# Two score batches of 224 and 288 key columns for query tiles 3 and 4, and row sums and a PSUM tile shared by two query tiles

## The chip, the core and the metric

The kernel runs on one core of one Trainium2 chip. The metric is the device time of one execution in microseconds (us). The engines are named as in the profile: PE is TensorE's matmuls and PEld its weight loads, DVE is VectorE, ACT is ScalarE, POOL is GpSimd, SP is SyncE, which only issues DMAs here.

## The reference

Attention with a memory, and behind it a feed-forward layer with a squared ReLU. B=4 batches, H=8 heads, S=576 tokens, D=64.

```
scores = q @ k.T / sqrt(D), masked causally (keys after the query get -1e9)
a      = exp(scores - rowmax);  a /= rowsum(a) + 1e-9
local  = a @ v
phi(x) = where(x > 0, x, exp(x) - 1) + 1
mem    = (phi(q) @ M_prev) / (phi(q) @ z_prev + 1e-6)
g      = sigmoid(beta)                        # one number per head
attn   = g * mem + (1 - g) * local
x      = attn.transpose(0, 2, 1, 3).reshape(2304, 512)
out    = relu(x @ w_in) ** 2 @ w_out          # w_in 512 x 2048, w_out 2048 x 512
```

## The kernel before

Queries come in tiles: tile 0 with 64 tokens, tiles 1 to 4 with 128 each. Tile 0 of all batches is done apart, at the start. Keys of tile 3 reach to column 448, of tile 4 to 576, of tile 2 to 320 and of tile 1 to 192.

`attention()` is a generator for one unit: a batch, a pair of heads and some tiles. Batches 0 and 1 are cut into units with tiles 1 and 2 and units with tiles 3 and 4 (four of each in a batch); batches 2 and 3 have four units each with all four tiles. These are 24 units, numbered here 0 to 23. Units 0 to 2 transpose in float32 on PE (`full`), units 0 to 5 compute scores with one matmul term, the 18 from unit 6 on with three terms (high times high, low times high, high times low).

What one unit does, in the order of its lines:

- It splits q and k into high and low parts (L475 to L478), applies phi (L488 to L502), scales v into the float16 pair `vs` (L525, L528), multiplies phi(q) by the memory into `pm` and writes g times the memory's answer into `feat` (L552 to L558). `feat` is the attention's output and the feed-forward's input.
- `scores(group)` computes one batch of scores into `sps`, a PSUM tile of 2 heads by 512 columns (tag "s", one buffer). `SGROUP` says which columns of which tile form a batch, in tuples (tile, first key, last key). The matmuls are at L583. Then DVE takes each head's part of each tuple out of PSUM (L604: scale, mask, running minimum `mx`) into the float32 tile `e`. A part that doesn't begin at key 0 takes `mx` of the first part as its start (a column of one number per partition). Only when the last part is out can the next batch be written.
- For each tile in the order 2, 1, 3, 4: ACT takes the exponential of `e` in place, one instruction for each head, and writes the row's sum into `sm` (L624; a tile of 128x2, tag "sm", four buffers, one tile for each query tile). ACT makes the float16 high part of `a` (L662), DVE the low part (L664), SP issues a transposing DMA `aT<-a` (L668). DVE adds 1e-9 to `sm` and multiplies it by `vz` (L669) and takes the reciprocal (L673).
- PE multiplies `aT` by `vs` into `acc` (L688; PSUM, tag "av", two buffers, used also for `pm` and `vt`). DVE adds the product times `sm` to `feat`, once for each head (L691, 128x64).

`moe(n)` is the feed-forward for 256 tokens: 24 "up" matmuls of 256 columns for each of eight pairs of feature blocks (L973 to L975), ReLU and square on ACT (L979, L980), a float16 high part `gh` on ACT (L982) and a low part `gl` on DVE (L985), and 12 "down" matmuls of 512 columns (L944 to L946). Its input `xT` is made of `feat` by `token_halves` (L715 to L724, with a transposing DMA). The last 512 tokens go through `moe_last` (L744), after all attention; matmuls of 512 tokens into `seven` (L812 to L814, L841).

The order of instructions isn't written by hand: a scheduler with a model of times places the instructions of all generators on the engines' queues, so the feed-forward's matmuls fill PE between the attention's. Score matmuls have a high priority in it. What is queued on one engine runs in that order. A change in `attention()` therefore moves other instructions too.

Of the kernel before, what the change touches and what calls it, by code (L numbers as in the profile page):

```python
# [8 lines left out]
F32 = mybir.dt.float32  # L9
# [6 lines left out]
ALU = mybir.AluOpType  # L16
# [50 lines left out]
TORD = [2, 1, 3, 4]  # L67
SGROUP = {2: [[(2, 0, 320), (1, 0, 192)]], 1: [], 3: [[(3, 0, 448), (4, 0, 64)]], 4: [[(4, 64, 576)]]}
GB = 2
# [29 lines left out]
def fused_kernel(ctx: ExitStack, tc: tile.TileContext, t0_d, kk_d, qv_d, beta, w_in, w_out, out):  # L99
# [353 lines left out]
    def attention(b, p, tiles, ld, after, early, sfull, full, ap, ap_early):  # L453
# [113 lines left out]
        if ap_early:  # L567
            yield "whole"
        started, a12 = set(), None
        row = {}  # L570

        def scores(group):
# [20 lines left out]
            for (i, ka, kb), cs in zip(group, at_col):  # L593
                q0 = QT[i][0]
                if ka == 0:
                    row[i] = (
                        ap.tile([P, 2, S], F32, tag="e", name="e", bufs=EB if ap is at else EB2),
                        at.tile([P, 2, 2], F32, tag="mx", name="mx", bufs=4),
                        at.tile([P, 2], F32, tag="sm", name="sm", bufs=4),
                    )  # L600
                e, mx, _ = row[i]
                s = int(ka > 0)
# [12 lines left out]
        for i in [t for t in TORD if t in tiles]:  # L615
            q0, n = QT[i]
            ke = q0 + n
            for group in SGROUP[i]:
                scores(group)
            ns = 2 if any(ka for g in SGROUP[i] for t, ka, _ in g if t == i) else 1  # L620
            e, mx, sm = row.pop(i)
            for h in range(2):
# [24 lines left out]
            else:  # L647
# [20 lines left out]
                nc.sync.dma_start_transpose(out=aT[:, :, :n], in_=a[:n])  # L668
            nc.vector.scalar_tensor_tensor(  # L669
                out=sm[:n], in0=sm[:n], scalar=1e-9, in1=gm[:n, h0 : h0 + 2] if full else vz[:n],  # L670
                op0=ALU.add, op1=ALU.mult,
            )
            nc.vector.reciprocal(sm[:n], sm[:n])  # L673
            yield

            acc = ps.tile([P, 2, D], F32, tag="av", name="acc", bufs=2)
            for h in range(2):
# [9 lines left out]
                for x, (lhs, rhs) in enumerate(mms):  # L687
                    nc.tensor.matmul(acc[:n, h], lhs[:, :n], rhs, start=x == 0, stop=x == len(mms) - 1)  # L688
            for h in range(2):
                xo = memx[:n, i - 1, h]  # L690
                x = nc.vector.scalar_tensor_tensor(  # L691
                    out=xo, in0=acc[:n, h], scalar=sm[:n, h : h + 1], in1=xo, op0=ALU.mult, op1=ALU.add
                )
                step.setdefault(me, x)
            yield
# [446 lines left out]
```

## Time and profile before

| | |
|---|---|
| times of 3 runs | 562.0, 559.24, 561.57 us |
| median | 561.57 us |
| the profiled execution | 561.7 us |
| its span (first to last instruction) | 559.9 us |
| outside the span | 1.8 us |
| busy in the span | PE 522.5 us (93%), PEld 369.5 (66%), DVE 451.9 (81%), ACT 412.0 (74%), POOL 17.8 (3%) |
| mean granted clock of TensorE | 0.976 of full speed |

The page also gives the span in 40 slices of 14 us with each engine's busy tenths: up to about 136 us PE stands at 5 to 9, from there on nearly always at 9; DVE is at 8 or 9 up to 255 us, and at 6 to 8 after that; the attention ends at about 437 us, and from there to the end PE has only the feed-forward. The clock that the throttle granted PE is given in tenths of full speed in these slices and in windows as a share (1.00 is full speed).

How the rows below are to be read. A row of a timeline is a run of equal instructions: start in us from the span's start, us from the first's start to the last's end, engine, line, operation, out<-in tiles, shape and count; in square brackets the idle time of the engine before it, and what ended that. Instructions on one engine overlap at their ends, so the cost of one is read from its start to the next one's start, where the next waits for nothing.

### The profile page before, as it was taken

The page shows a single profiled execution, that of the slowest core. Times are in us where ns is not written, and L with a number is a line of the kernel's source. Part 1 is how long each engine was busy: PE and PEld are TensorE (multiplying, and loading weights), DVE is VectorE, ACT ScalarE, POOL GpSimd, SP SyncE. Part 2 cuts the span into 40 slices and gives each one's busy share as a digit, 9 for nine tenths or more (in the row PEclk, how much of TensorE's full clock was granted, in tenths as well). Part 3 has the DMA queues.
Part 4 walks back from the last instruction along what each step waited for, and adds up shares of the span by engine and source line. Part 5 has one row for each costly group of instructions (what it writes and reads, how often), then busy time and mean ns, then how long its engine had stood idle before and what let it go on. Part 6 is the DMA issues. An engine that isn't in the chain of part 4 may idle for free.

```text
span 559.9 us, 12611 instructions
## 1 busy us (share of the span) xinstructions
PE 522.5 (93%) x4767; PEld 369.5 (66%) x4767; DVE 451.9 (81%) x1421; ACT 412.0 (74%) x884; POOL 17.8 (3%) x20
## 2 busy tenths in 40 slices
PE   5655999998999999999989999999999999999996
PEld 4544766656777767667756777667766866447766
DVE  6898879998997999999967778888686788745645
ACT  3699997894788879989867777889666734566252
POOL 1000030111010000000000000000000000000000
PEclk9967999998999999999989999999999999999999
DMA  8968931497576759988746476481755320100002
GB/s 309 405 215 247 325 109 39 124 160 186 117 157 152 174 136 158 179 171 183 131 90 150 115 138 123 76 145 47 115 94 80 91 39 1 39 1 1 1 1 75
DMA packets 133132, 71.37 MB, mean 127 GB/s; under 512 B 115408, under 2 KB 121552, under 8 KB 133072
## 3 DMA queue, kind: packets, MB, share of 16 engines
q1 hardware_dynamic: 133072, 70.57, 53.7%
q8 instruction: 37, 0.61, 0.5%
q14 instruction: 23, 0.19, 0.1%
HBM read 37.53 MB, written 4.72 MB: 75 GB/s over the span
## 4 chain that ended last, share of the span: by engine, by line
PE 53%; DVE 23%; ACT 11%; DMA 9%; issue 2%; SPq 0%; POOL 0%; DVEq 0%; ACTq 0%
PE up L973 6%; PE up L974 5%; PE up L975 5%; DVE e L604 5%; PE oacc L945 5%; PE oacc L946 5%; PE oacc L944 5%; PE acc L688 4%; DVE a L664 4%; PE seven L841 4%; ACT e L624 3%; PE sp L583 3%; DMA xT<-hl 2%; PE seven L814 2%; PE seven L813 2%; PE seven L812 2%
## 5 line engine op out<-in xcount | busy, mean ns | idle before, releaser
L973 PE MATMUL up<-xT,w 128*128 128x256 f16 x448 | 124.0, 277 | 5.7 <-DMA xT<-hl 5.1
L974 PE MATMUL up<-xT,w 128*128 128x256 f16 x448 | 123.9, 277 | 0.0
L975 PE MATMUL up<-xT,w 128*128 128x256 f16 x448 | 123.8, 276 | 0.0
L624 ACT ACTIVATE e<-e,mx 128x320 f32<-128x320 f32 (+3 forms) x128 | 77.4, 606 | 40.4 <-DVE feat L691 22.3
L944 PE MATMUL oacc<-w,gh 128*128 128x512 f16 x224 | 85.2, 380 | 0.6 <-ACT gh L982 0.5
L945 PE MATMUL oacc<-w,gh 128*128 128x512 f16 x224 | 85.3, 381 | 0.0
L946 PE MATMUL oacc<-w,gl 128*128 128x512 f16 x224 | 81.6, 380 | 0.0
L664 DVE SCALAR_TENSOR_TENSOR a<-e,a 128x128 f16<-128x128 f32 x116 | 65.8, 578 | 10.4 <-ACT a L662 9.5
L662 ACT ACTIVATE a<-e 128x128 f16<-128x128 f32 x116 | 55.0, 523 | 1.8 <-DMA aT<-a 1.4
L973 PEld LDWEIGHTS <-w 128*128 128x128 f16 x448 | 44.4, 99 | 16.3 <-DMA xT<-hl 5.6
L974 PEld LDWEIGHTS <-w 128*128 128x128 f16 x448 | 44.5, 99 | 11.5 <-issue 1.1
L975 PEld LDWEIGHTS <-w 128*128 128x128 f16 x448 | 44.5, 99 | 8.5 <-issue 0.4
L604 DVE CUSTOM_DVE_ANT_0 e<-sp,mask 128x320 f32<-128x320 f32 (+3 forms) x128 | 47.3, 422 | 2.7 <-PE sp L583 2.7
L979 ACT ACTIVATE r<-up,gam 128x512 f32<-128x512 f32 x48 | 32.4, 675 | 23.0 <-PE up L975 20.4
L688 PE MATMUL acc<-vs,aT 128*128 128x64 f16 x1138 | 43.8, 194 | 4.6 <-DMA aT<-a 3.2
L688 PEld LDWEIGHTS <-aT 128*128 128x128 f16 x1138 | 39.9, 99 | 10.1 <-DMA aT<-a 4.4
L985 DVE TENSOR_TENSOR gl<-r,gh 128x512 f16<-128x512 f32 x56 | 38.5, 688 | 5.8 <-ACT gh L982 5.3
L944 PEld LDWEIGHTS <-gh 128*128 128x128 f16 x224 | 22.0, 98 | 22.5 <-ACT gh L982 0.9
L946 PEld LDWEIGHTS <-gl 128*128 128x128 f16 x224 | 21.8, 98 | 22.3 <-DVE gl L985 0.5
L841 PEld LDWEIGHTS <-g 128*128 128x128 f16 x336 | 32.7, 98 | 5.4 <-DVE g L767 1.3
L980 ACT ACTIVATE r<-r 128x512 f32<-128x512 f32 x56 | 34.9, 624 | 0.6
L945 PEld LDWEIGHTS <-gh 128*128 128x128 f16 x224 | 22.0, 98 | 20.0 <-issue 0.3
(192 smaller groups left out, 1038.3 us busy)
## 6 DMA issues: line engine op xcount, KB each, us to landing
raw<-in_w_in_dram SPq DMA_DIRECT2D x16, 512.0 KB, 6.6
raw<-in_w_out_dram SPq DMA_DIRECT2D x16, 512.0 KB, 7.5
vv<-in_qv_dram SPq DMA_DIRECT2D x16, 320.0 KB, 3.1
kd<-in_kk_dram SPq DMA_DIRECT2D x16, 288.0 KB, 3.1
out_dram<-o SPq DMA_DIRECT2D x12, 256.0 KB, 2.1
qm<-in_qv_dram SPq DMA_DIRECT2D x8, 321.0 KB, 3.0
qm<-in_qv_dram SPq DMA_DIRECT2D x8, 193.0 KB, 4.0
vv<-in_qv_dram SPq DMA_DIRECT2D x8, 192.0 KB, 3.3
```

What stands on the lines that cost most here:

```text
L604: nc.vector.tensor_tensor_reduce(out=e[:, h, ka:kb], in0=sps[:, h, cs], in1=mask[:, 448 - q0 + ka : 448 - q0 + kb], scale=-0.125, scalar=3 ...
L624: ex = nc.scalar.activation(e[:n, h, :ke], e[:n, h, :ke], AF.Exp, bias=bs, scale=-1.0, accum_out=sm[:n, h : h + 1])
L662: nc.scalar.mul(av[:, :, o0 : o0 + w], x, SC)
L664: nc.vector.scalar_tensor_tensor(out=av[:, :, o0 + w : o0 + 2 * w], in0=x, scalar=SC, in1=av[:, :, o0 : o0 + w], op0=ALU.mult, op1=ALU.sub ...
L688: nc.tensor.matmul(acc[:n, h], lhs[:, :n], rhs, start=x == 0, stop=x == len(mms) - 1)
L841: mms.append(nc.tensor.matmul(x[:, blk], g[j][:, i0, a, blk, p], t_side(j, p, m, i1), start=j == js[0] and p == n == 0, stop=j == js[-1] a ...
L944: nc.tensor.matmul(acc[t], gh[:, u, ts], w_out_op(f, 0), start=f == f0, stop=False)
L945: nc.tensor.matmul(acc[t], gh[:, u, ts], w_out_op(f, 1), start=False, stop=False)
L946: nc.tensor.matmul(acc[t], gl[:, u, ts], w_out_op(f, 0), start=False, stop=f == f1)
L973: nc.tensor.matmul(uo, w_in_op(f, k, 0), x_op(k, 0), start=k == 0, stop=False)
L974: nc.tensor.matmul(uo, w_in_op(f, k, 0), x_op(k, 1), start=False, stop=False)
L975: nc.tensor.matmul(uo, w_in_op(f, k, 1), x_op(k, 0), start=False, stop=k == NK - 1)
```

## The change

The score batches of tiles 3 and 4 are cut otherwise: (3, keys 0 to 224) with (4, keys 0 to 288), then (3, 224 to 448) with (4, 288 to 576), and both batches come before tile 3's exponentials. Before, they were (3, 0 to 448) with (4, 0 to 64), then tile 3's softmax, then (4, 64 to 576) and tile 4's. Tiles 1 and 2 keep their one batch of 320 and 192 columns. In all units but the three `full` ones, tiles 1 and 2 share one `sm` tile of 128x2x2, and tiles 3 and 4 another; L669 and L673 run once on it, when the second tile's exponentials are there. The two tiles share one PSUM tile `acc` of 128x2x2x64, and `feat` is updated once for both: DVE multiplies `acc` by `sm` in place (a tensor_tensor with `sm` broadcast along the columns, 128x256), and adds it to `feat` (128x256). The `sm` and `acc` tiles have as many buffers as before, four and two.

```diff
-SGROUP = {2: [[(2, 0, 320), (1, 0, 192)]], 1: [], 3: [[(3, 0, 448), (4, 0, 64)]], 4: [[(4, 64, 576)]]}
+SGROUP = {2: [[(2, 0, 320), (1, 0, 192)]], 1: [], 3: [[(3, 0, 224), (4, 0, 288)], [(3, 224, 448), (4, 288, 576)]], 4: []}
...
-                        at.tile([P, 2], F32, tag="sm", name="sm", bufs=4),
...
-            ns = 2 if any(ka for g in SGROUP[i] for t, ka, _ in g if t == i) else 1
-            e, mx, sm = row.pop(i)
+            ns = len([t for g in groups.values() for x in g for t, *_ in x if t == i])
+            e, mx = row.pop(i)
+            ts = [i] if full else [i, i + 1] if i % 2 else [i - 1, i]
+            done = i in (1, 4) or len(ts) == 1
+            if ts[0] not in sums:
+                sums[ts[0]] = at.tile([P, len(ts), 2], F32, tag="sm", name="sm", bufs=4)
+            sm2, at_t = sums[ts[0]], i - ts[0]
+            sm = sm2[:, at_t]
...
-            nc.vector.scalar_tensor_tensor(
-                out=sm[:n], in0=sm[:n], scalar=1e-9, in1=gm[:n, h0 : h0 + 2] if full else vz[:n],
-                op0=ALU.add, op1=ALU.mult,
-            )
-            nc.vector.reciprocal(sm[:n], sm[:n])
-            yield
-            acc = ps.tile([P, 2, D], F32, tag="av", name="acc", bufs=2)
+            if done:
+                g2 = (gm[:, h0 : h0 + 2] if full else vz)[:, None].to_broadcast([P, len(ts), 2])
+                nc.vector.scalar_tensor_tensor(out=sm2, in0=sm2, scalar=1e-9, in1=g2, op0=ALU.add, op1=ALU.mult)
+                rc = nc.vector.reciprocal(sm2, sm2)
+            yield
+            if ts[0] not in prods:
+                prods[ts[0]] = ps.tile([P, len(ts), 2, D], F32, tag="av", name="acc", bufs=2)
+            acc = prods[ts[0]]
...
-                    nc.tensor.matmul(acc[:n, h], lhs[:, :n], rhs, start=x == 0, stop=x == len(mms) - 1)
-            for h in range(2):
-                xo = memx[:n, i - 1, h]
-                x = nc.vector.scalar_tensor_tensor(
-                    out=xo, in0=acc[:n, h], scalar=sm[:n, h : h + 1], in1=xo, op0=ALU.mult, op1=ALU.add
-                )
-                step.setdefault(me, x)
+                    mm = nc.tensor.matmul(acc[:, at_t, h], lhs[:, :n], rhs, start=x == 0, stop=x == len(mms) - 1)
+            if done:
+                to = memx[:, ts[0] - 1 : ts[-1]]
+                if len(ts) == 1:
...
+                else:
+                    nc.vector.tensor_tensor(
+                        out=acc, in0=acc, in1=sm2[:, :, :, None].to_broadcast([P, 2, 2, D]), op=ALU.mult
+                    )
+                    step.setdefault(me, rc)
+                    nc.vector.tensor_tensor(out=to, in0=acc, in1=to, op=ALU.add)
```

`step` is what a unit two further on waits for with its loads; it is the unit's first `feat` update before, the first reciprocal now. There are 29 pairs of tiles outside the `full` units, and 16 units with tiles 3 and 4, 14 of them with three terms of scores.

On ACT, in one of the units with all four tiles, tile 3's two exponentials (128x448) were followed by tile 3's `a` and by feed-forward work, and six rows stood between them and tile 4's exponentials (128x576). `r` and `gh` are the feed-forward's.

```order
L624 ACTIVATE e,sm<-e,mx 128x448 x2
L662 ACTIVATE a<-e 128x2x64
L662 ACTIVATE a<-e 128x2x384
L979 ACTIVATE r<-up,gam 128x512
L980 ACTIVATE r<-r 128x512
L982 CAST gh<-r 128x512
L525 ACTIVATE vs<-vv,vy 128x10x64
L624 ACTIVATE e,sm<-e,mx 128x576 x2
```

In the changed kernel, in such a unit, both tiles' exponentials stand in a row, and both tiles' `a` behind them (L631, L669 and L996 to L999 are the former L624, L662 and L979 to L982).

```order
L631 ACTIVATE e,sm<-e,mx 128x448 x2
L631 ACTIVATE e,sm<-e,mx 128x576 x2
L669 ACTIVATE a<-e 128x2x64
L669 ACTIVATE a<-e 128x2x384
L996 ACTIVATE r<-up,gam 128x512
L669 ACTIVATE a<-e 128x2x64
L669 ACTIVATE a<-e 128x2x512
L997 ACTIVATE r<-r 128x512
L999 CAST gh<-r 128x512
L631 ACTIVATE e,sm<-e,mx 128x320 x2
```

What moved: four exponentials come together, and tile 3's `a` now stands behind tile 4's exponentials.

On DVE, between two batches of scores of such a unit, before: the last part of a batch leaves PSUM (L604), the `feat` updates of two earlier tiles, tile 3's `sm` and `a`, a feed-forward `gl`, then the first part of the next batch.

```order
L604 ISA e,mx<-sp,mask 128x64
L604 ISA mx 128x1
L691 SCALAR_TENSOR_TENSOR feat<-acc,sm,feat 128x64 x4
L669 SCALAR_TENSOR_TENSOR sm<-sm,vz 128x2
L673 RECIPROCAL sm<-sm 128x2
L664 SCALAR_TENSOR_TENSOR a<-e,a 128x2x64
L664 SCALAR_TENSOR_TENSOR a<-e,a 128x2x384
L985 TENSOR_TENSOR gl<-r,gh 128x512
L604 ISA e,mx<-sp,mask,mx 128x512
```

In the changed kernel, behind a batch of tiles 2 and 1 (L671 is the former L664, L707 and L711 are the new update of `feat`):

```order
L604 ISA e,mx<-sp,mask 128x192
L604 ISA mx 128x1
L671 SCALAR_TENSOR_TENSOR a<-e,a 128x2x64
L707 TENSOR_TENSOR acc<-acc,sm 128x256
L679 RECIPROCAL sm<-sm 128x4
L671 SCALAR_TENSOR_TENSOR a<-e,a 128x2x384
L494 SCALAR_TENSOR_TENSOR qm<-pe,qm 128x512
L711 TENSOR_TENSOR feat<-acc,feat 128x2x2x64
```

What moved: the four updates of `feat` became two wider instructions, set apart by others, and one reciprocal serves two tiles.

On PE the feed-forward's work was dealt out anew. Behind the last product of `aT` with `vs` stand 178 up and 96 down matmuls before the change and 308 and 168 after it; the sums over the program are 1344 and 672 in both. So 130 ups and 72 downs that stood beside the attention now stand behind it.

## Rows read from the trace of the kernel before

**Rows 1.** Windows: us, busy us (instructions) PE, PEld, DVE, ACT, POOL; PEclk, DMA share, GB/s.

```profile
136.00:427.00 291.00, 286.92 (x2913) 206.38 (x2910) 247.33 (x908) 234.75 (x544) 3.63 (x4) 0.99 0.65 130
204.00:255.00 51.00, 50.88 (x503) 35.49 (x504) 48.70 (x168) 44.05 (x95) 0.00 (x0) 1.00 0.84 164
280.00:300.00 20.00, 18.12 (x177) 12.78 (x176) 15.10 (x52) 12.87 (x29) 0.00 (x0) 0.91 0.51 105
```

**Rows 2.** Timeline of PE, products with v: start, us, in brackets the idle before.

```profile
281.44 0.82 PE L688 MATMUL acc<-vs,aT 128*128 128x64 f16 x22
284.13 1.67 PE L688 MATMUL acc<-vs,aT 128*128 128x64 f16 x28 [1.88 <-DMA aT<-a]
...
350.36 0.82 PE L688 MATMUL acc<-vs,aT 128*128 128x64 f16 x22 [0.64 <-DMA aT<-a]
...
418.43 0.76 PE L688 MATMUL acc<-vs,aT 128*128 128x64 f16 x20 [0.63 <-DMA aT<-a]
```

**Rows 3.** Waits from 255 to 437 us: engine, line, releaser, total, times, longest.

```profile
ACT e L624 <- DVE feat L691: 22.3, 14, 3.3
DVE sm L669 <- ACT e L624: 15.4, 20, 1.5
```

**Rows 4.** The chain, PE's pieces: start, us to the next piece, line.

```profile
160.34 0.95 PE sp L583 x12
...
290.26 0.89 PE sp L583 x6
...
308.62 1.07 PE sp L583 x12
```

**Rows 5.** Timeline of DVE, scores leaving PSUM, parts of 448, 64 and 512 columns.

```profile
330.25 0.62 DVE L604 CUSTOM_DVE_ANT_0 e<-sp,mask 128x448 f32<-128x448 f32 x1
...
330.79 0.62 DVE L604 CUSTOM_DVE_ANT_0 e<-sp,mask 128x448 f32<-128x448 f32 x1
...
331.34 0.22 DVE L604 CUSTOM_DVE_ANT_0 e<-sp,mask 128x64 f32<-128x64 f32 x1
...
331.48 0.22 DVE L604 CUSTOM_DVE_ANT_0 e<-sp,mask 128x64 f32<-128x64 f32 x1
...
337.21 0.74 DVE L604 CUSTOM_DVE_ANT_0 e<-sp,mask,mx 128x512 f32<-128x512 f32 x1
...
337.88 0.75 DVE L604 CUSTOM_DVE_ANT_0 e<-sp,mask,mx 128x512 f32<-128x512 f32 x1
```

**Rows 6.** Timeline of DVE, reciprocal and updates of feat.

```profile
319.63 0.41 DVE L558 TENSOR_TENSOR feat<-pm,nm 128x256 f32<-128x256 f32 x1
319.96 0.16 DVE L673 RECIPROCAL sm<-sm 128x2 f32<-128x2 f32 x1
320.03 0.41 DVE L558 TENSOR_TENSOR feat<-pm,nm 128x256 f32<-128x256 f32 x1
...
325.19 0.86 DVE L691 SCALAR_TENSOR_TENSOR feat<-acc,sm,feat 128x64 f32<-128x64 f32 x4
325.96 0.69 DVE L985 TENSOR_TENSOR gl<-r,gh 128x512 f16<-128x512 f32 x1
```

**Rows 7.** Timeline of PE, one down matmul and two ups in a row.

```profile
164.18 0.38 PE L946 MATMUL oacc<-w,gl 128*128 128x512 f16 x1
164.39 0.27 PE L973 MATMUL up<-xT,w 128*128 128x256 f16 x1
164.50 0.27 PE L974 MATMUL up<-xT,w 128*128 128x256 f16 x1
```

**Rows 8.** Timelines of PE and DVE: two batches' first matmul, and what stands behind their last part on DVE.

```profile
208.80 0.50 PE L583 MATMUL sp<-kh,qh 64*128 64x512 f32 x2
...
211.18 0.47 DVE L691 SCALAR_TENSOR_TENSOR feat<-acc,sm,feat 128x64 f32<-128x64 f32 x2
...
238.57 0.47 PE L583 MATMUL sp<-kh,qh 64*128 64x448 f32 x2
...
244.35 0.19 DVE L552 SCALAR_TENSOR_TENSOR nm<-pm,gi 128x4 f32<-128x4 f32 x1
```

More of the change, by code (lines that the diff above doesn't have):

```diff
@@ L568, in attention @@
             yield "whole"
-        started, a12 = set(), None
+        groups = SGROUP
+        started, a12, sums, prods = set(), None, {}, {}
         row = {}
@@ L598, in scores @@
                         at.tile([P, 2, 2], F32, tag="mx", name="mx", bufs=4),
-                        at.tile([P, 2], F32, tag="sm", name="sm", bufs=4),
                     )
-                e, mx, _ = row[i]
+                e, mx = row[i]
                 s = int(ka > 0)
@@ L617, in attention @@
             ke = q0 + n
-            for group in SGROUP[i]:
+            for group in groups[i]:
                 scores(group)
-            ns = 2 if any(ka for g in SGROUP[i] for t, ka, _ in g if t == i) else 1
-            e, mx, sm = row.pop(i)
+            ns = len([t for g in groups.values() for x in g for t, *_ in x if t == i])
[6 more added lines that the diff above has]
+            sm = sm2[:, at_t]
             for h in range(2):
@@ L687, in attention @@
                 for x, (lhs, rhs) in enumerate(mms):
-                    nc.tensor.matmul(acc[:n, h], lhs[:, :n], rhs, start=x == 0, stop=x == len(mms) - 1)
-            for h in range(2):
-                xo = memx[:n, i - 1, h]
-                x = nc.vector.scalar_tensor_tensor(
-                    out=xo, in0=acc[:n, h], scalar=sm[:n, h : h + 1], in1=xo, op0=ALU.mult, op1=ALU.add
-                )
-                step.setdefault(me, x)
+                    mm = nc.tensor.matmul(acc[:, at_t, h], lhs[:, :n], rhs, start=x == 0, stop=x == len(mms) - 1)
+            if done:
+                to = memx[:, ts[0] - 1 : ts[-1]]
+                if len(ts) == 1:
+                    for h in range(2):
+                        x = nc.vector.scalar_tensor_tensor(
+                            out=to[:, 0, h], in0=acc[:, 0, h], scalar=sm[:, h : h + 1], in1=to[:, 0, h],
+                            op0=ALU.mult, op1=ALU.add,
+                        )
+                        step.setdefault(me, x)
+                else:
+                    nc.vector.tensor_tensor(
+                        out=acc, in0=acc, in1=sm2[:, :, :, None].to_broadcast([P, 2, 2, D]), op=ALU.mult
+                    )
+                    step.setdefault(me, rc)
+                    nc.vector.tensor_tensor(out=to, in0=acc, in1=to, op=ALU.add)
             yield
```

## The prediction

> **What bounds the kernel now.** I read the page's slices first, then windows, then PE's timeline, then the waits, and DVE's timeline last. The slices and the windows answer where PE is full. From 136 to 427 us, the part in which attention and feed-forward share the engines, PE is busy 286.92 of 291 us, while DVE has 247.33 (85%) and ACT 234.75 [rows 1]. So what a change gives there must be PE work or a PE wait, and what it costs on DVE or ACT counts only if PE comes to wait for it. Between 204 and 255 us DVE is busy 48.70 of 51 us (95.5%), and PE still lacks only 0.12 us [rows 1]: DVE nearly full is not yet a PE that waits.
>
> PE's timeline from 136 to 437 us then shows the few waits there are. Three stand before products with v, for the transposing DMA: 1.88 at 284.13, 0.64 at 350.36 and 0.63 at 418.43, 3.15 us together [rows 2]. After the first the clock falls: from 280 to 300 us it was granted at 0.91 of full speed, which is 20 x 0.09 = 1.8 us lost, and what PE did before was to stand idle for these 1.88 us [rows 1, 2]. The table of waits says how the transposes come late: ACT's exponentials wait 22.3 us, 14 times, for a `feat` update on DVE [rows 3]. An exponential writes `sm`, and a unit of four tiles takes all four `sm` buffers, so the exponential of a tile stands until the `feat` update of the tile four before it has read its sums. DVE's `sm` work in turn waits 15.4 us for the exponential [rows 3].
>
> **The change part by part.**
>
> *Score batches on PE.* A batch of 448 and 64 columns takes 1.07 us, one of 512 takes 0.89, one of 320 and 192 takes 0.95 [rows 4]. No row has 224 and 288; it is bounded by 0.89 and 1.07. I take the row nearest in its cut, 0.95. A unit with tiles 3 and 4 then goes from 1.07 + 0.89 = 1.96 to 1.90, and 14 such units with three terms give -0.8 us. By the ends of the bound it is -2.5 to +2.5 us. This lies on the path, since PE is the bound.
>
> *Scores leaving PSUM on DVE.* From start to start, 448 columns take 0.54 us, 64 take 0.14, and 512 with a start read from a column 0.67 [rows 5]. That is 0.08 us and 1.04 ns a column, and 0.055 more for the column. So 224 and 288 take 0.31 and 0.38, with the column 0.37 and 0.43. A unit goes from 2 x (0.54 + 0.14 + 0.67) = 2.70 to 2 x (0.31 + 0.38 + 0.37 + 0.43) = 2.98, and 16 units give +4.5 us of DVE.
>
> *Sums and `feat` on DVE.* A reciprocal costs 0.07 us to the next start, at most its own 0.16 [rows 6]. With the L669 of equal size, 116 of them become 58, which is -4.1 us (to -9). Four `feat` updates take 0.77 us [rows 6]. The two of 256 columns that replace them have no row of their own; the nearest is L558, 256 columns out of PSUM, 0.33 from start to start and 0.41 by itself [rows 6]. With 0.33 each, and 0.06 since the second waits for the first, they take 0.72; with 0.41 each, 0.82. I take 0.72: 29 x -0.05 = -1.5 us (to +1.5). In sum DVE gets 4.5 - 4.1 - 1.5 = -1.1 us: as good as unchanged.
>
> *The four `sm` buffers.* They now hold eight tiles, so an exponential stands behind the sums of two units, not one, and the 22.3 us of ACT's wait goes. What is late next is not the exponential but DVE, below. In the new order the distance between a tile's scores and its products with v is longer in the units of four tiles, so I take the three waits of 3.15 us and the 1.8 us of clock as gone: -4.9 us. If the transposes are as late as before it is 0. The update of `feat` for a pair comes when the second tile's products are done; nothing reads `feat` earlier than the unit's end, so the delay hides behind the feed-forward that PE has in hand.
>
> *What the new order moves.* 130 ups and 72 downs go from beside the attention to behind it. An up costs 0.11 us and a down 0.21 [rows 7], together 14.3 + 15.1 = 29.4 us of PE. As PE's work it is the same total and costs nothing. But it was the cover for DVE: the attention's part is now 291 - 0.8 - 4.9 - 29.4 = 255.9 us long on PE, and DVE's work there is 247.33 - 1.1 less the `gl` of these downs (12 downs go with one `gl` of 0.61, so 3.7), which makes 242.5 us, or 95%. That is the load of the stretch from 204 to 255 us, but now for the whole part. There PE didn't wait, because it had other work between the batches of scores; the next batch needs the PSUM tile that DVE empties. In that stretch a batch begun at 208.80 was out at 211.18 (2.4 us), and one begun at 238.57 only at 244.35 (5.8 us) [rows 8]. So PE needs 2.4 to 5.8 us of its own work from one batch's start to the next one's. In the new order, from unit 6 on, six distances hold under 5 us of PE's work (before: two of 39). The tightest lies between the last batch of unit 17 and the first of unit 18: the batch 0.95, five ups and five downs 1.6, and 28 products of 0.82 / 22 = 0.037 each [rows 2], in sum 3.6 us. A wait at such a place is from 0 to 5.8 - 3.6 = 2.2 us; for the mean delay of 4.1 us it is 0.5. I take 0.6 at each of the six, a little more because DVE is this full throughout: +3.6 us (0 to 13).
>
> The Trainium skill ("Perfetto Trace Analysis", section "Identifying the Most-Contended Engine") says that the busy share is a fair measure for VectorE, and that for TensorE the weight loads' share is to be taken in place of the matmuls'. By it DVE with 95.5% binds the stretch from 204 to 255 us, and PE, whose loads take 35.49 of 51 us (70%), does not [rows 1]. The trace disagrees for that stretch, since PE had no wait in it; by the page the changed kernel would come out as in the slow rival below.
>
> **The sum.** 559.9 (span) - 0.8 - 4.9 + 3.6 = 557.8, and 1.8 outside the span: 559.6 us. That execution took 561.7, 0.1 over the median of 561.57, so I compare with the median as it is.
>
> **The rivals.**
>
> *PE stays the bound (faster).* If DVE's idle share stays at the 4.5% of the stretch from 204 to 255 us, its 242.5 us take 254 us, less than PE's 255.9, and the new waits are 1 us at most: 557.0 us. For it: PE's 0.12 us of waits there. Against it: six tight distances where that stretch had none.
>
> *DVE becomes the bound (slower).* PE's queue is in order: a batch of scores that waits for its PSUM tile holds up the feed-forward and the products behind it, DVE then lacks their results, and no backlog is left to make it good. It decides as soon as DVE is idle more than 5% of the attention's part. Its price: the wider pair at 0.82 instead of 0.72 in the 26 pairs from unit 6 on, 2.6 us, gives 245.1 of DVE; idle 6.5%, two points over the best stretch, makes it 262.1 and so 6.2 us over PE's 255.9; and two waits of the length that lowered the clock before cost 2 x 1.8 = 3.6. So 554.2 + 6.2 + 3.6 + 1.8 = 565.8, and 567.2 with DVE idle 7%. For it: the delay that grew to 5.8 us within one stretch [rows 8]. Against it: DVE's lead can wander without PE seeing it.
>
> *The change doesn't do what it says.* If the batches cost 1.07 like the uneven one, they take 2.14 for 1.96, +2.5 instead of -0.8, and if the transposes are late as before, 4.9 come back. Each alone gives 563 to 564.5 us, both 567.8. For it: the `feat` update that the exponentials wait for stands itself in DVE's queue behind other work, and that work stays. Against it: 14 waits of up to 3.3 us on one and the same releaser [rows 3] are what a buffer looks like. It belongs to the cases "same" and "slower".
>
> **How the numbers follow.** 0.5% (2.8 us) is about what a measurement of this kernel can tell from no change, so faster means under 558.8 us and slower over 564.4. The forecast of 559.6 with its spread up to 564.4 has 0.38. Faster has 0.36: the rival at 557.0 (0.26), and the forecast's sum with cheaper sums and batches (0.10). Slower has 0.26: DVE as bound (0.20), and the change that doesn't work (0.06). The range runs from 554.0, where the new waits are nothing and a batch takes 0.89 (557.0 - 1.0 - 1.7 = 554.3), to 567.5, which takes in the slow rival; the tail above, an order that makes PE wait at each unit, and the one below hold 2 in 10.
>
> **What would show it.** The waits of exponentials for `feat` are gone from the table, and the three waits for the transposes with them; if not, the step on buffers was wrong. A batch of 224 and 288 at 0.95 us in the chain. Parts of 224 and 288 at 0.31 to 0.43 on DVE; L707 and L711 at 0.33 to 0.41. DVE busy about 95% in the attention's part, which ends some 30 us earlier. PE's waits for `mx`/`e` of L604 before scores: 1 us means the fast rival, 4 the forecast, 8 and a clock under 0.97 the slow one. The prediction is wrong if the attention's part shows long PE waits that it doesn't name, as for `feat` by way of `xT`, or for products in units 6 to 8, where the new order has the shortest distances from scores to products.

## The result and the profile after

The changed kernel takes 563.88 us (median; 562.66 to 565.52) against 560.73 for the kernel before, measured side by side. The ratio is 1.0059, with a 95% interval of 1.0043 to 1.0075: slower by 0.6%. That is just past the 0.5% that the prediction called a difference, and the interval reaches under it. The forecast was 559.6 us and no difference. The profiled execution took 563.82 us with a span of 562.0.

Windows of the changed kernel, with the columns of [rows 1]; the last row runs to the end of the span:

```profile
136.00:427.00 291.00, 283.47 (x3023) 205.91 (x3020) 257.53 (x902) 240.59 (x561) 3.48 (x4) 1.00 0.68 139
204.00:255.00 51.00, 49.30 (x529) 36.34 (x528) 50.12 (x178) 46.56 (x103) 0.00 (x0) 1.00 0.80 170
280.00:300.00 20.00, 19.65 (x182) 13.10 (x183) 16.75 (x61) 15.77 (x38) 0.00 (x0) 1.00 0.69 140
136.00:562.00 426.00, 413.62 (x3894) 290.69 (x3890) 326.43 (x999) 300.35 (x641) 3.48 (x4) 1.00 0.48 100
```

The same stretch, from 136 us to the end, in the kernel before:

```profile
136.00:559.90 423.90, 415.26 (x3815) 290.96 (x3811) 333.37 (x1047) 302.83 (x642) 3.63 (x4) 1.00 0.49 99
```

These two rows hold the result of the profiled executions. PE is busy 1.6 us less (415.26 to 413.62), and not busy 3.7 us more (423.90 - 415.26 = 8.6, 426.00 - 413.62 = 12.4): the stretch is 2.1 us longer, as the span is. The gains came, and more was lost to waits. From 204 to 255 us DVE is 98% busy, and PE now lacks 1.70 us where it lacked 0.12 [rows 1].

The timeline of PE shows where (answering [rows 2]; start, us, in brackets the idle before and what ended it):

```profile
157.06 0.99 PE L696 MATMUL acc<-vs,aT 128*128 128x64 f16 x28 [1.28 <-DMA aT<-a]
...
217.15 0.55 PE L696 MATMUL acc<-vs,aT 128*128 128x64 f16 x13 [0.59 <-DMA aT<-a]
...
242.63 0.52 PE L696 MATMUL acc<-vs,aT 128*128 128x64 f16 x12 [1.11 <-DMA aT<-a]
...
278.98 0.99 PE L696 MATMUL acc<-vs,aT 128*128 128x64 f16 x28 [0.46 <-DMA aT<-a]
...
338.74 1.43 PE L696 MATMUL acc<-vs,aT 128*128 128x64 f16 x43 [0.77 <-DMA aT<-a]
...
365.67 0.39 PE L961 MATMUL oacc<-w,gh 128*128 128x512 f16 x1 [1.19 <-ACT gh L999]
...
398.21 1.98 PE L696 MATMUL acc<-vs,aT 128*128 128x64 f16 x62 [0.95 <-DMA aT<-a]
```

And the table of waits from 136 to 437 us (answering [rows 3]; total, times, longest):

```profile
DVE sm L678 <- ACT e L631: 5.9, 8, 1.7
ACT e L631 <- DVE mx L604: 5.6, 4, 2.2
...
PE acc L696 <- DMA aT<-a: 5.2, 6, 1.3
```

The exponentials' 22.3 us of waits for `feat` are gone, as forecast. The products' waits for the transposing DMA are not: six of 5.2 us in place of three of 3.2, which is 2.0 of the 3.7 us. Another 1.2 us are one wait of a down matmul for `gh`, at 365.67; on ACT's queue that `gh`, begun at 365.00, stands behind four exponentials from 361.29 us on and the four parts of `a` that follow them. Each wait is 1.3 us at most, and none of them cost clock: from 280 to 300 us it is 1.00 where it was 0.91 [rows 1].

### The profile page after: what moved, and what is told of

Read it like the earlier page. It is cut to its first block, busy times and chain, and to the rows that moved or that the text cites. A ratio compares the mean times of both kernels' runs of the same rounds, so it can differ in the third digit from the quotient of the medians.

```text
span 562.0 us, 12760 instructions
## 1 busy us (share of the span) xinstructions
PE 519.9 (93%) x4859; PEld 369.1 (66%) x4859; DVE 443.7 (79%) x1369; ACT 409.9 (73%) x884; POOL 18.2 (3%) x20
## 4 chain that ended last, share of the span: by engine, by line
PE 42%; DVE 22%; ACT 20%; DMA 11%; issue 3%; SPq 1%; POOL 0%; ACTq 0%; DVEq 0%
ACT e L631 5%; DVE e L604 5%; PE oacc L962 5%; PE oacc L963 5%; PE oacc L961 5%; PE up L990 5%; PE up L992 4%; PE up L991 4%; PE acc L696 4%; DVE a L671 4%; DMA aT<-a 3%; PE seven L858 3%; ACT a L669 3%; DVE g L784 2%; DMA raw<-in_w_in_dram 2%
## 5 line engine op out<-in xcount | busy, mean ns | idle before, releaser
L631 ACT ACTIVATE e<-e,mx 128x320 f32<-128x320 f32 (+3 forms) x128 | 77.2, 608 | 7.8 <-DVE mx L604 5.6
L671 DVE SCALAR_TENSOR_TENSOR a<-e,a 128x128 f16<-128x128 f32 x116 | 63.3, 563 | 8.0 <-ACT a L669 7.8
L996 ACT ACTIVATE r<-up,gam 128x512 f32<-128x512 f32 x48 | 32.6, 680 | 42.4 <-PE up L992 41.2
L669 ACT ACTIVATE a<-e 128x128 f16<-128x128 f32 x116 | 54.0, 521 | 3.0 <-DMA aT<-a 3.0
L991 PEld LDWEIGHTS <-w 128*128 128x128 f16 x448 | 44.4, 99 | 12.6 <-issue 2.4
L604 DVE CUSTOM_DVE_ANT_0 e<-sp,mask 128x320 f32<-128x320 f32 (+3 forms) x128 | 47.7, 416 | 0.2 <-PE sp L584 0.2
L696 PE MATMUL acc<-vs,aT 128*128 128x64 f16 x1138 | 40.4, 193 | 7.1 <-DMA aT<-a 5.2
L696 PEld LDWEIGHTS <-aT 128*128 128x128 f16 x1138 | 37.1, 98 | 10.7 <-DMA aT<-a 6.7
L784 DVE TENSOR_TENSOR gf<-gf 128x512 f32<-128x512 f32 x16 | 10.8, 688 | 33.1 <-ACT gf L834 33.0
L961 PEld LDWEIGHTS <-gh 128*128 128x128 f16 x224 | 21.9, 98 | 22.1 <-ACT gh L999 2.1
```

The costliest lines, as they stand in the source:

```text
L604: nc.vector.tensor_tensor_reduce(out=e[:, h, ka:kb], in0=sps[:, h, cs], in1=mask[:, 448 - q0 + ka : 448 - q0 + kb], scale=-0.125, scalar=3 ...
L631: ex = nc.scalar.activation(e[:n, h, :ke], e[:n, h, :ke], AF.Exp, bias=bs, scale=-1.0, accum_out=sm[:n, h : h + 1])
L669: nc.scalar.mul(av[:, :, o0 : o0 + w], x, SC)
L671: nc.vector.scalar_tensor_tensor(out=av[:, :, o0 + w : o0 + 2 * w], in0=x, scalar=SC, in1=av[:, :, o0 : o0 + w], op0=ALU.mult, op1=ALU.sub ...
L696: mm = nc.tensor.matmul(acc[:, at_t, h], lhs[:, :n], rhs, start=x == 0, stop=x == len(mms) - 1)
L961: nc.tensor.matmul(acc[t], gh[:, u, ts], w_out_op(f, 0), start=f == f0, stop=False)
```

## One wait, followed back

The wait of 1.11 us before 242.63 can be followed in rows of three engines. First ACT's `a` (both parts of tile 4's, 64 and 512 columns of each head; the row names the first one's shape), then DVE's timeline, then the chain's DMA and product:

```profile
233.38 1.24 ACT L669 ACTIVATE a<-e 128x128 f16<-128x128 f32 x2
...
234.05 0.38 DVE L604 CUSTOM_DVE_ANT_0 e<-sp,mask 128x224 f32<-128x224 f32 x1
...
234.36 0.38 DVE L604 CUSTOM_DVE_ANT_0 e<-sp,mask 128x224 f32<-128x224 f32 x1
...
234.67 0.45 DVE L604 CUSTOM_DVE_ANT_0 e<-sp,mask 128x288 f32<-128x288 f32 x1
...
235.05 0.45 DVE L604 CUSTOM_DVE_ANT_0 e<-sp,mask 128x288 f32<-128x288 f32 x1
...
235.43 0.68 DVE L494 SCALAR_TENSOR_TENSOR qm<-pe,qm 128x512 f32<-128x512 f32 x1
236.03 0.28 DVE L671 SCALAR_TENSOR_TENSOR a<-e,a 128x128 f16<-128x128 f32 x1
236.24 0.42 DVE L707 TENSOR_TENSOR acc<-acc,sm 128x256 f32<-128x256 f32 x1
236.57 0.28 DVE L515 TENSOR_REDUCE vy<-vt 128x1 f32<-128x128 f32 x1
236.77 1.21 DVE L671 SCALAR_TENSOR_TENSOR a<-e,a 128x1024 f16<-128x1024 f32 x1
...
238.01 4.58 DMA aT<-a
242.63 0.20 PE acc L696
```

ACT is done with tile 4's `a` at 234.6. DVE, which never pauses here, reaches its low part 2.2 us later, at 236.77, since four parts of scores, phi and the former pair's product stand ahead of it. The DMA then takes 4.58 us, and PE comes to the products 1.11 us before it lands. The transposing DMAs are not slower than they were, 4.2 us by the median from issue to landing after 4.3. Two things are left that can be at fault: DVE is too full, or the products stand too early on PE's queue. The experiments had to tell these apart.

The same rows price the parts: 224 columns take 0.31 us from start to start, 288 take 0.38, and L707 takes 0.33, as the prediction had them.

## The experiments

Three ideas stood at the start: that DVE's load sets the time once the feed-forward has moved behind the attention (A), that the new cut of the batches is what harms (B), and that each new order is a mere draw (C). Four kernels do one part of the change each.

**The new batches alone.**

```diff
-SGROUP = {2: [[(2, 0, 320), (1, 0, 192)]], 1: [], 3: [[(3, 0, 448), (4, 0, 64)]], 4: [[(4, 64, 576)]]}
+SGROUP = {2: [[(2, 0, 320), (1, 0, 192)]], 1: [], 3: [[(3, 0, 224), (4, 0, 288)], [(3, 224, 448), (4, 288, 576)]], 4: []}
...
-            ns = 2 if any(ka for g in SGROUP[i] for t, ka, _ in g if t == i) else 1
+            ns = len([t for g in SGROUP.values() for x in g for t, *_ in x if t == i])
```

> The kernel before with the new score batches alone; sums, PSUM tile and feat update stay one per query tile. Behind the attention's last product its PE order has 99 ups and 92 downs (30.7 us; before 40.2, after the change 69.9). Theory A (the part of the attention is as long as DVE lets it be; PE's waits grow with the feed-forward work that has moved behind the attention): more cover than before, so no slower than before, 558 to 562 us, and the exponentials wait for feat as before (some 20 us). Theory B (the cut is what harms: both batches ahead of the exponentials make the transposes late): 563 us or more. Theory C (each new order is a draw, with no pattern): anything within 3 us of before.

562.89 us, 1.0027 [1.0011, 1.0043]. The exponentials wait 6.7 us for `feat`, not some 20.

**The sharing alone, with the old batches** (the same line the other way, in the changed kernel).

> The changed kernel with the old score batches: sums, PSUM tile and feat update shared by two tiles. Behind the last product stand 322 ups and 180 downs (74.0 us). Theory A: as dense as the changed kernel or denser, though DVE has 4.5 us less to do: 562 to 565 us, DVE over 95% busy from 200 to 255 us, and waits of products for transposes of 4 us or more from 136 us on. Theory B: faster than before, about 557 us. Theory C: within 3 us of before.

579.47 us, 1.0325 [1.0299, 1.0352]. The products' waits for the transposing DMA are 3.2 us, not 4 or more, so they don't explain the loss.

**Eight `sm` buffers in the kernel before.**

```diff
-                        at.tile([P, 2], F32, tag="sm", name="sm", bufs=4),
+                        at.tile([P, 2], F32, tag="sm", name="sm", bufs=8),
```

> The kernel before with eight buffers of sm in place of four, and nothing else. Behind the last product stand 218 ups and 132 downs (52.3 us). All theories: the 22 us of exponentials waiting for feat are gone. Theory A: halfway between, DVE about 90% busy in the attention's part; with the waits for transposes gone 557 to 560 us. Theory B: the same gain, 556 to 558 us. Theory C: within 3 us of before, either way.

572.80 us, 1.0216 [1.0192, 1.0241]. The exponentials' wait for `feat` isn't gone, as was expected, but 6.3 us of it are left.

**Both: new batches and eight `sm` buffers, nothing shared.**

> The new score batches with eight buffers of sm, sums and feat update one per tile. Behind the last product stand 219 ups and 132 downs (52.4 us), as with eight buffers alone. Theory A: as with eight buffers alone within 2 us, DVE 4.5 us busier and PE 0.8 us less busy. Theory B: slower by 4 us or more than eight buffers alone. Theory C: no relation between the two.

560.19 us, 0.9999 [0.9969, 1.0028].

All three ideas fall as they were put. Where most of the exponentials' wait is taken away, which the prediction counted as a gain, the time rises by 11 to 18 us with the old batches, while with the new ones it falls by 2.7 us (eight buffers) or rises by 1.0 (sharing). The new batches cost 0.3% by themselves, but beside eight buffers or sharing they gain 12.6 and 15.6 us, so they are not what harms (B). A draw of 3 us doesn't reach 18 (C); a wider draw isn't excluded by this. And two orders with the same 52 us of feed-forward behind the attention differ by 12.6 us (A). What comes in the place of the wait shows in the table of waits of the kernel with eight `sm` buffers:

```profile
DVE a L664 <- ACT a L662: 26.2, 30, 4.4
...
ACT a L662 <- DMA aT<-a: 14.7, 8, 3.2
...
PE sp L583 <- DVE mx L604: 4.1, 5, 1.8
```

ACT may not write the next `a` while a DMA still transposes the one before out of the same tile. DVE's low part of `a` stands behind that, the score parts stand behind it on DVE's queue, and PE's next batch waits for them: the slow rival's path, started by another buffer. One instance in its timelines:

```profile
264.97 1.04 ACT L662 ACTIVATE a<-e 128x128 f16<-128x128 f32 x2 [2.43 <-DMA aT<-a]
...
265.31 0.29 DVE L664 SCALAR_TENSOR_TENSOR a<-e,a 128x128 f16<-128x128 f32 x1 [2.05 <-ACT a L662]
...
268.40 0.41 PE L583 MATMUL sp<-kh,qh 64*128 64x320 f32 x2 [0.78 <-DVE mx L604]
```

In the kernel before, the wait for `sm` seems to have kept the exponentials back until the `a` tiles were free: ACT's wait for the DMA is 0.6 us there, 3.0 in the changed kernel, and none of note with new batches and eight buffers. The run after the next diff, with that wait gone and the order unchanged, bears this out: 7.1 us.

The next kernels hold each engine's instructions in a given order: each instruction gets an order-only dependency on the one that precedes it in another kernel's list.

```diff
...
+    for rows in want.values():
+        at = [have[f"I-{x}"] for x in rows if f"I-{x}" in have]
+        for a, b in zip(at, at[1:]):
+            tc.add_manual_dep(b, a.name, AFTER, reason="the order of another kernel")
```

In the traces each held kernel runs every engine's instructions in the order that it was to have. No kernel was held unchanged in its own order, so what the holding by itself does to the time isn't measured; differences of a few tenths of a percent between a held and a free kernel carry that doubt.

**Eight `sm` buffers in the order of the kernel before.**

> Eight buffers of sm, and each engine's instructions held in the order of the kernel before. The same freeing with the order of its own cost 11 us. Theory D (the freeing is worth something by itself, and what costs is the order that is laid out once the wait is gone, in which exponentials and what follows them are packed closer than the transposing DMAs allow): no slower than before, 556 to 561.5 us, the exponentials' 22 us of waits for feat gone, PE's three waits for transposes (3.2 us) down to 1 or less. Theory F (the wait itself paced ACT usefully; without it ACT runs ahead into other waits in any order): 565 us or more.

560.35 us, 0.9977 [0.9954, 1.0000]. The same buffers cost 11 us in the order that the scheduler makes for them, and nothing, perhaps a gain of 0.2%, in the old one. The products' waits for the DMA were expected at 1 us or less and are 2.4. The other waits move here as well, without reaching PE:

```profile
ACT e L624 <- DVE mx L604: 22.9, 21, 2.1
DVE a L664 <- ACT a L662: 17.5, 23, 2.5
...
ACT a L662 <- DMA aT<-a: 7.1, 4, 2.8
...
PE acc L688 <- DMA aT<-a: 2.4, 3, 1.8
```

So it is the order, not the freed buffer as such.

**A second `a` tile in the two slow kernels, each held in its own order** (16 blocks, in the pool of every other unit).

```diff
-                    a = ap.tile([P, tg * P], F16, tag=f"a{tg}", name="a")
+                    a = ap.tile([P, tg * P], F16, tag=f"a{tg}", name="a", bufs=2 if tg == 16 and ap is not at else 1)
```

> Eight buffers of sm in the order that this kernel makes (572.8 us), with a second buffer of the 16-block tile a in every other unit's pool (memory holds no more). Theory D with the a tiles as the next scarce thing (ACT's a waits 14.7 us for the transposing DMA that still reads the tile): that wait falls to about half, DVE's wait for a from 26 us to about 15, and the time by 3 to 7 us, to 566 to 570 us. If the a tiles are not the cause, 572 to 573 us and the waits turn up elsewhere.

569.84 us, 1.0131 [1.0087, 1.0175], from 1.0216.

> Old score batches with sums and PSUM tile shared by two tiles, in the order of that kernel (579.5 us), with the same second buffer of a in every other unit's pool. With the a tiles as the next scarce thing: ACT's wait of 9.8 us for the transposing DMA falls to about half, and the time by 2 to 6 us, to 573 to 577 us. If not: 579 us.

577.73 us, 1.0270 [1.0222, 1.0318], from 1.0325; these intervals overlap, and ACT's wait fell only from 9.8 to 7.1 us, not to half. In the kernel with eight `sm` buffers ACT's wait has nearly halved (14.7 before):

```profile
ACT a L662 <- DMA aT<-a: 8.0, 6, 2.5
```

The `a` tile is a cause in the first, for 3 us by the medians and 5 by the ratios, of 11 to 12, with the tile doubled in half of the units. In the second the gain is near the bound of what was expected, and most of its 18 us is not explained by it.

**The changed kernel in its own order, with less work on DVE.** The addition covers one column in 64. The multiplication still writes `acc`, not `feat` as the expectation says, so what is left out of most of the result is the softmax's share of the attention and not the memory's; DVE's work is the same either way.

```diff
-                    nc.vector.tensor_tensor(out=to, in0=acc, in1=to, op=ALU.add)
+                    nc.vector.tensor_tensor(out=to[:, :, :, :1], in0=acc[:, :, :, :1], in1=to[:, :, :, :1], op=ALU.add)
```

> The changed kernel in its own order of instructions, but the second of the two new feat instructions adds 4 of its 256 columns, and the first writes to feat: the memory's share of the attention is left out, and DVE has about 7.9 us less to do (29 x 0.27). Theory A (DVE's load is what makes PE wait): PE's waits from 136 us on, 8.5 us in the changed kernel, fall to 4 or less, 557 to 560 us. Theory E (not DVE's load but the way from exponentials by a and the transposing DMA to the products, laid out too short): the waits for transposes stay at 4 to 5 us and the time at 562 to 564 us.

562.83 us, 1.0014 [0.9991, 1.0037]. That is 1 us (by the medians) to 2.5 us (by the ratios) less than the changed kernel for 8 us of DVE work. By the profile it is next to nothing: the span is 561.7 after 562.0, and the products' waits for the DMA are 6.3 us in its table. DVE's load counts for a part at most.

**The waiting products later on PE's queue.** In the changed kernel and in the kernel before, each otherwise in its own order, the next ups or downs are pulled ahead of the products that waited. No instruction is added.

> The changed kernel with every engine held in its own order, except that on PE seven groups of products which waited (127.56, 157.06, 217.15, 242.63, 278.98, 338.74 and 398.21 us; 7.1 us in sum) stand behind the next 6 to 12 ups or downs, 1.3 to 2.3 us of feed-forward pulled ahead of each. Theory E (these products stand too early on PE's queue for the way through ACT, DVE and the transposing DMA): the waits go and the time falls by 5 to 7 us, to 557 to 559 us, under the kernel before. Theory A (DVE and ACT are the bound, and PE only shows it): the waits turn up at the next product or batch, 562 to 564 us.

561.28 us, 1.0017 [0.9997, 1.0037]: 0.4%, some 2.5 us, back from 1.0059, half of the least that was expected. The products' waits are down to 0.7 us,

```profile
PE acc L696 <- DMA aT<-a: 0.7, 1, 0.7
```

but other waits grew by 2 us: PE is not busy for 10.1 us from 136 us on, after 12.4.

```profile
136.00:559.10 423.10, 412.97 (x3898) 291.09 (x3894) 327.00 (x999) 300.21 (x641) 3.48 (x4) 1.00 0.49 101
```

> The kernel before, held in its own order, except that the three product groups that waited for a transposing DMA (284.13, 350.36 and 418.43 us; 3.15 us and 1.8 us of clock behind the first) stand behind the next 7 to 12 ups or downs. The prediction's price for these waits is 4.9 us: 556 to 557 us. If the pulled downs wait in turn for their gl, or the clock falls without the wait too: 559 to 561 us.

559.59 us, 0.9976 [0.9959, 0.9993]: 1.4 us, where the prediction had priced the same three waits and the clock behind the first at 4.9. In its trace the waits are down to 0.4 us, and the clock from 280 to 300 us is 1.00.

**Which half of the sharing.** Four narrow updates of `feat` in place of the two wide instructions, the rest as in the changed kernel:

```diff
-                    nc.vector.tensor_tensor(
-                        out=acc, in0=acc, in1=sm2[:, :, :, None].to_broadcast([P, 2, 2, D]), op=ALU.mult
-                    )
-                    step.setdefault(me, rc)
-                    nc.vector.tensor_tensor(out=to, in0=acc, in1=to, op=ALU.add)
+                    for x in range(2):
+                        for h in range(2):
+                            nc.vector.scalar_tensor_tensor(
+                                out=to[:, x, h], in0=acc[:, x, h], scalar=sm2[:, x, h : h + 1], in1=to[:, x, h],
+                                op0=ALU.mult, op1=ALU.add,
+                            )
+                    step.setdefault(me, rc)
```

> The changed kernel with four feat updates of 64 columns for a pair (each multiplies and adds) in place of the two of 256; sums and PSUM tile stay shared. Its order is its own (288 ups and 165 downs behind the last product; the changed kernel 308 and 168). If the two wide instructions are where the loss is: 561 us or less. If it is the sharing of the PSUM tile or the sums: 563 to 566 us.

559.81 us, 0.9980 [0.9957, 1.0003].

With a PSUM tile and an update for each query tile, the sums still shared:

```diff
-                prods[ts[0]] = ps.tile([P, len(ts), 2, D], F32, tag="av", name="acc", bufs=2)
-            acc = prods[ts[0]]
+            acc = ps.tile([P, 2, D], F32, tag="av", name="acc", bufs=2)
+            prods[i] = acc
...
-                else:
-                    nc.vector.tensor_tensor(
-                        out=acc, in0=acc, in1=sm2[:, :, :, None].to_broadcast([P, 2, 2, D]), op=ALU.mult
-                    )
-                    step.setdefault(me, rc)
-                    nc.vector.tensor_tensor(out=to, in0=acc, in1=to, op=ALU.add)
```

> The changed kernel with a PSUM tile of products and a feat update for each query tile; the sums stay shared by two tiles. Behind the last product stand 127 ups and 92 downs (33.7 us; changed kernel 69.9, new batches with eight sm buffers 52.4). If the shared PSUM tile is what sets the changed kernel apart from the new batches with eight sm buffers (560.2 us): 559 to 561 us. If the shared sums do: 563 us or more.

559.92 us, 0.9977 [0.9962, 0.9992].

Either way 4 us are back, which would lay the loss on the two wide instructions, were it not that each kernel has an order of its own. So each program was run in the other's order.

> The changed kernel, every engine held in the order that the kernel with four feat updates made (559.8 us): the two wide instructions stand where the first and the last of the four stood. If the two wide instructions themselves cost the 4 us between that kernel and the changed one (563.9 us): 563 us or more. If it is the order that the scheduler laid out around them: 559 to 561 us.

559.83 us, 0.9979 [0.9955, 1.0002]. This is the changed kernel's work in full, with its wide instructions, in another order: it is 4 us faster than the changed kernel, and equal to the narrow one.

> The kernel with four feat updates, every engine held in the changed kernel's order: the four stand where the addition stood. If the instructions cost the 4 us: 560 us. If the order does: 563 to 565 us.

568.50 us, 1.0122 [1.0086, 1.0158]. The narrow updates are not faster in the changed kernel's order, they are 4.6 us slower, more than was expected. PE isn't busy for 15.6 us from 136 us on, after 12.4, and has a wait for the score parts that the changed kernel hasn't in this stretch:

```profile
PE sp L584 <- DVE mx L604: 1.3, 2, 1.1
```

Why slower and not equal isn't settled: all four stood here where the addition had stood, later than the multiplication.

So the wide instructions cost nothing against the narrow ones in the good order, and the same wide instructions cost 4 us more in the order that the scheduler made for them: the 4 us lie in the order. The place followed above looks like this in the good order, with PE's row of the same products behind DVE's of tile 4's low part:

```profile
238.29 1.22 DVE L671 SCALAR_TENSOR_TENSOR a<-e,a 128x1024 f16<-128x1024 f32 x1
...
245.14 0.28 PE L696 MATMUL acc<-vs,aT 128*128 128x64 f16 x4
246.30 0.87 PE L696 MATMUL acc<-vs,aT 128*128 128x64 f16 x24
```

DVE is no earlier here (238.29; 236.77 in the changed kernel). But PE reaches the products 6.9 us behind the start of the low part, not 4.8, and waits for nothing. Over the whole stretch that is a part of it alone: the products still wait 3.5 us for the DMA, after 5.2, and PE isn't busy for 9.1 us, after 12.4:

```profile
136.00:556.70 420.70, 411.60 (x3872) 289.65 (x3870) 326.88 (x994) 299.45 (x639) 3.47 (x4) 1.00 0.49 101
```

**Two buffers of the shared sums.** The thought was that buffers which make the scheduler wait keep the order loose.

```diff
-                sums[ts[0]] = at.tile([P, len(ts), 2], F32, tag="sm", name="sm", bufs=4)
+                sums[ts[0]] = at.tile([P, len(ts), 2], F32, tag="sm", name="sm", bufs=2)
```

> The changed kernel with two buffers of the shared sums in place of four, which hold four tiles as before the change; the order is laid out anew, with 238 ups and 145 downs behind the last product (57.3 us; changed kernel 69.9). If the waits that the buffers set keep the order loose, as in the kernel before: PE's waits for transposes from 136 us on fall under 3 us and the time to 559 to 561 us, though the exponentials wait for DVE again. If not: 563 us or more.

584.04 us, 1.0387 [1.0337, 1.0437]: the worst of all, and the thought falls. The exponentials wait for the pair's update, and the transposes come late behind them:

```profile
PE acc L696 <- DMA aT<-a: 13.0, 10, 3.1
ACT e L631 <- DVE acc L707: 11.2, 7, 4.9
```

**A faster version.** The kernel with narrow updates in its order, with its five waiting groups of products moved later:

> The kernel with four feat updates (559.8 us), held in its order, except that on PE the five product groups that waited (157.53, 219.83, 231.75, 234.30 and 280.93 us; 3.3 us in sum) stand behind the next 5 to 14 ups or downs. By what the same move gave in the changed kernel (7.1 us of waits moved, 2.6 us gained) and in the kernel before (3.15 and 1.4): 1.2 to 1.5 us, 558.3 to 558.6 us, which would be 0.5% under the kernel before. If the waits turn up elsewhere: 559.8 us.

557.97 us, 0.9937 [0.9913, 0.9961], under both kernels. Where the gain over its parent comes from isn't shown: from 136 us on PE is not busy for 8.7 us in either, and the products' waits are 2.3 us, after 3.3. From 136 us to the end of its span of 555.2:

```profile
136.00:555.20 419.20, 410.51 (x3858) 287.92 (x3856) 325.88 (x1044) 298.75 (x639) 3.47 (x4) 1.00 0.49 101
```

## Why the prediction was wrong, step by step

- *Score batches on PE: right.* A batch of 224 and 288 columns takes 0.93 us in the chain of the changed kernel, where 0.95 was taken from the batch of 320 and 192:

```profile
248.74 0.93 PE sp L584 x12
```

- *Scores leaving PSUM, sums and `feat` on DVE: right* to 0.02 us for each instruction. The 0.06 us for the addition that waits for the multiplication had no row; where one stands right behind the other, 0.46 us lie between their starts, not 0.39. And the sum was mis-sized: DVE is busy 443.7 us over the span, after 451.9 us, 8.2 less where 1.1 was forecast. So PE came to wait more beside a DVE with less to do. Whether two wide instructions or four narrow ones update `feat` made no difference in the good order; in the changed kernel's order the four were slower.
- *The four `sm` buffers: half right.* The wait for `feat` went, with no trace of it left. What the prediction put next, DVE's queue, is one of two things that came: with the old batches and eight buffers it was the `a` tile that a DMA still reads. The prediction didn't look for other buffers on the same path.
- *The waits for the transposes: wrong, and this step decides.* They and the clock behind the first were taken as gone, -4.9 us, since the distance between a tile's scores and its products had grown. They are six, 5.2 us, in place of three, 3.2. The distance was counted on PE alone. The way from scores to products runs through four exponentials in a row on ACT (the excerpt of ACT's order shows tile 3's `a` behind tile 4's exponentials), through DVE's queue and through a DMA of 4.6 us, and the backlog on those was not counted into it. (That this way, laid out too short, is the cause was tested by moving the products: 2.5 of the 5 to 7 us that were expected came back.) The prediction had followed that backlog (5.8 us, [rows 8]) to the PSUM tile of the scores only. Its last sentence had named products in units 6 to 8 as a place to look: one of the six waits, 1.28 us at 157.06, is unit 6's; the others come in units 12 to 22.
- *The price of these waits: mis-sized.* Moving the three in the kernel before gave 1.4 us, not 4.9. The 1.8 us of clock were taken as the price of a wait of 1.88 us, but they didn't always follow one: with eight buffers in the order of the kernel before, PE waits 1.77 us before the same products, and from 280 to 300 us the clock is 1.00. And in the changed kernel with its products moved, a freed microsecond of PE was in part spent at another wait.
- *New waits before score batches: wrong in place.* 3.6 us were forecast at six tight distances. PE's only listed wait for L604 is at 118 us, ahead of that part:

```profile
118.02 1.13 PE L584 MATMUL sp<-kd,qm 64*128 64x224 f32 x8 [0.97 <-DVE mx L604]
```

- *The order moved 29 us behind the attention: right.* Its last `feat` update is at 408.8 us, 28 us earlier. That this makes DVE decisive was the slow rival; it named the mechanism in part (DVE 98% busy from 200 to 255 us, PE's waits up), but its exit, the score batch, and its price of 6 us with two falls of the clock were wrong. Its load was mis-sized too: from 136 us to the end of the attention DVE is busy 241.3 of 273 us (88%), not 95%. The part is 17 us longer than forecast: for 10 of them the prediction had let it end at 427 us, where the attention of the kernel before ended at 437, and the rest are gains that didn't come and new waits.

In sum: forecast from 136 us on were 2.6 us less of PE work (0.8 of batches, 1.8 of clock) and about as many waits as before; measured were 1.6 us less work and 3.7 us more waits. That the time stayed within the forecast's range is owed to the range, which took in the slow rival, and not to its mechanism.

The measured cause is the order: the changed kernel's work takes 563.9 us in one order and 559.8 in another, and with narrow updates and five groups moved 558.0. What in the order costs it is shown for about half: moving the products that waited gave 2.5 us. What stays open: the rest of it, why the scheduler's order differs in that way between wide and narrow updates, and most of the 18 us that the sharing costs with the old batches.

## What to carry to other kernels

Where a scheduler lays out the queues anew, a change is two changes, the work and the order. Price the work from rows, and test the order by itself by holding each program in the other's order, before an instruction is blamed or praised. And before a wait is counted as a gain, look for the next buffer on the same path: here the tile that a transposing DMA reads was kept free by the wait that was removed (ACT's wait for it went from 0.6 to 7.1 us in one and the same order).

## What the runs showed of the hardware

- The length of a wait didn't say whether the granted clock falls. Waits of 0.5 to 1.3 us of PE left it at 1.00 in the changed kernel, from 136 us on. One of 1.88 us in the kernel before was followed by 0.91 over 20 us [rows 1, 2], and one of 1.86 us in the kernel with eight `sm` buffers stands in a window with 0.97 (first PE's row, then the window):

```profile
336.24 2.00 PE L688 MATMUL acc<-vs,aT 128*128 128x64 f16 x34 [1.86 <-DMA aT<-a]
```

```profile
320.00:380.00 60.00, 58.05 (x559) 41.79 (x559) 49.29 (x182) 50.01 (x113) 0.00 (x0) 0.97 0.51 102
```

But one of 1.88 us in the changed kernel's work in the good order left it at 1.00:

```profile
156.59 0.99 PE L696 MATMUL acc<-vs,aT 128*128 128x64 f16 x28 [1.88 <-DMA aT<-a]
```

```profile
150.00:170.00 20.00, 18.12 (x216) 13.75 (x215) 18.23 (x69) 17.06 (x43) 1.72 (x2) 1.00 0.81 172
```

- A tile that a transposing DMA reads can't be written again until the DMA has landed: 4.2 us by the median from issue to landing in the changed kernel, and in the kernel with eight `sm` buffers ACT stood 14.7 us for that.
